# A list scheduler's estimated durations replaced by repeat times, in a kernel of attention, four experts and a gated MLP

## The chip, the cores and the metric

The kernel runs on one core of a Trainium2 chip, in one launch. The metric is the device time of that launch in microseconds, the median of repeated runs. The engines are TensorE (PE; its weight loads are PEld), VectorE (DVE), ScalarE (ACT), GpSimd (POOL) and SyncE (SP), which issues DMAs. Each takes its instructions in program order and waits at semaphores for the others.

## The reference

Three layers follow one another, all in float32. 2 batches of 8 heads, 576 positions, head size 64; then 1152 tokens of 512 numbers.

```python
scores = scale * np.matmul(q, k.transpose(0, 1, 3, 2))
x = (log1p(abs(i - j)) / log1p(max(i, 1)))[..., None]
bias = np.maximum(x @ w1 + b1, 0.0) @ w2          # 32 hidden, one bias per head
attn = softmax(scores + bias); x = attn @ v       # tokens of 8 * 64 numbers
p = domain_probs / (domain_probs.sum(-1, keepdims=True) + 1e-09)
out += p[:, e:e + 1] * (np.maximum(x @ w1[e], 0.0) @ w2[e])   # for 4 experts, 1024 hidden
return ((x @ w_a) * (x @ w_b)) @ w_out            # 1536 hidden, weights in float64
```

## The kernel before

**Operands.** Most matrix products take each float32 operand as a high part and a rest (`hi`, `lo`; `wh`, `wl`; `hh`, `hl`) and add three products of the parts. ScalarE or VectorE makes the high part by a cast, VectorE or GpSimd the rest by a subtraction.

**The bias** (`bias_group`, lines 347 to 409). For each of 36 groups of 16 rows of positions, four operations make the hidden layer `hh` (line 356 on VectorE for three of them, line 358 on ScalarE for one), matmuls make `pb` (line 370), ScalarE or VectorE evacuates one side of it into `bst` (line 388 or 390), GpSimd or ScalarE mirrors the other side (line 395), and SyncE stores the rows in DRAM, `bias_d` (line 405). `bias_tile` (line 448) reads them back as tiles `bt` of 128 rows, two heads at a time. A tile needs all of its eight groups of rows.

**Attention** (`inputs`, `step`, `values`, `group`, lines 429 to 600). Two heads go together. `inputs` loads and splits q and k (lines 438 to 443). A step is a tile of 128 rows: matmuls `ps` (line 490), on VectorE a reduction that adds the bias and finds the row extreme (line 493), on ScalarE the exponential with a sum (line 503), transposes `pt` (line 516), copies into `ptb` (line 234, on ScalarE or VectorE), then for a group of steps the reciprocal sums spread by `rx`, `rp` and `rb` (lines 556 to 570), matmuls `pv` with v (line 581), and the attention's result as `x_hi` and `x_lo` (lines 587 to 590). The first two tiles of batch 0 (256 tokens) come first for all heads: the experts start on them.

**Experts** (`w1_item`, `w2_item`, lines 724 to 753). `up` (line 708) makes the hidden layer of 256 columns, ScalarE applies the relu (line 735), VectorE makes its rest (line 736), `down` (line 719) adds into banks `pz`. Pass 0 has the 256 first tokens, pass 1 all the others, which needs the whole attention. Weights come in 512 KB blocks: load `wst` (line 617), high part and rest (lines 618, 619).

**Gated MLP** (`convert`, `blocks64`, `x2_pair`, `ab_item`, `out_item`, lines 626 to 942). VectorE turns the float64 words into float32 (lines 636 to 657); a scheme with seven products in place of eight makes both up products (`pw`, `pr`, `pq`, line 842), with evacuations into `ct` between them; `out_item` multiplies by `w_out` and adds into `acc` (line 937).

**The order.** Nothing of this is issued as it is written. `op(...)` records an operation with its buffers, a rank (`prio`, lower first) and, for each engine that may do it, an estimated duration in ns. `Plan.run` (line 137) then simulates the engines with these estimates and emits the instructions in the order in which the simulated engines take them; on the chip each engine's queue keeps that order. The rules:

- An engine takes the ready operation of lowest rank, then of greatest age, whose buffers are free. An operation of rank under 0.9 is left to another engine if that one would finish it sooner (line 171).
- On TensorE, expert and MLP matmuls are fill (rank 2). While fill is ready, another matmul is taken only 300 ns after it became ready (MARGIN, line 165).
- A result counts as ready after the duration and a settling time of its engine (SETTLE, line 91).
- A DMA is put at its issue time plus 400 ns, or behind the DMA before it, plus its bytes at 250 per ns, and then 1500 ns more:

```python
dma = max(dma, now + ns + 400) + o.size / self.DMA_RATE
end = dma + self.DMA_LAT - 400
```

The estimates stand in `t_copy` (copies and casts from SBUF), `t_two` (two operands) and `t_psum` (one operand in PSUM), lines 237 to 247, and as numbers in the `op` calls.

Of the kernel before, what the change touches and what calls it, by code (L numbers as in the profile page):

```python
# [226 lines left out]
def tile_kernel(ctx, tc, qd, kd, vd, cst, probs, w1r, w2r, war, wbr, wor, out):  # L227
    nc = tc.nc
# [118 lines left out]
    def bias_group(u, rank):  # L347
# [3 lines left out]
        for g in range(4):  # L351
            G = 4 * u + g
            hh = new("hh")
            hs.append(hh)
            if g < 4 - acts:
                op({"DVE": n / 1.92 + 240}, lambda e, hh=hh, G=G: nc.vector.tensor_scalar(out=hh.t[:, :n], in0=tab[:, :n], scalar1=sc[:, G:G + 1], scalar2=negb, op0=ALU.mult, op1=ALU.max), r=[cs], w=[hh], prio=pri, lock=True)  # L356
            else:
                op({"ACT": n / 1.2 + 390}, lambda e, hh=hh, G=G: nc.scalar.activation(out=hh.t[:, :n], in_=tab[:, :n], func=AF.Relu, scale=sc[:, G:G + 1], bias=cw[:, 1:2]), r=[cs], w=[hh], prio=pri)
        pb = new("tv" if n <= 512 else "s", "pb")
# [11 lines left out]

        op({"PE": n * 1.9 + 350}, mm, r=[*hs, cs], w=[pb], hold=[bst], prio=pri)

# [25 lines left out]
        m = min(before, after - 1)  # L399
        side = op({e: v + 100 for e, v in t_psum(n, ENGINES["side"]).items()}, lambda e: put(e, *ends()[0]), r=[pb, cr], w=[bst], prio=pri)  # L400
        op({e: v for e, v in {"POOL": 2 * m + 150, "ACT": m / 1.2 + 280, "DVE": m / 0.96 + 200}.items() if e in ENGINES["mirror"].split()}, mirror, r=[pb, cr], w=[bst], after=[side], prio=pri)
# [67 lines left out]
    def step(m, b, t, k, q0, Q, K, ptb, sums):  # L469
# [3 lines left out]
        for s in range(2):  # L473
# [32 lines left out]
            if K.room is None:  # L506
                guests.append(o)
            red = op({"DVE": 840}, ttr, r=[ps, bt], hold=[pr, sums])
            if t < 4 or s == 1:
                exps.append(op({"ACT": 970}, ex, after=[red] if t < 4 else [red, half0], w=[sums], hold=[pr]))  # L510
            half0 = red
# [34 lines left out]
    def values(m, b, ts, w, V, ptb, sums):  # L546
# [35 lines left out]

        op({"PE": 10 * w + 350}, pvs, r=[ptb, V, rb], w=[pv], hold=[xf], prio=RANK["pv"])
        c = int(ts[0] > 1)
        o = xcol(b, c) + P * ts[0] - C0 * c
        o = slice(o, o + w)
        op({"DVE": w / 0.96 + 160}, lambda e: nc.vector.tensor_tensor(out=xf.t[:, :w], in0=pv.t[:, :w], in1=rb.t[:, :w], op=ALU.mult), r=[pv, rb], w=[xf], prio=RANK["fin"])
        hi = Buf(t=x_hi)
# [37 lines left out]
    def convert(src, whole):  # L626
# [3 lines left out]
        for h in range(2):  # L630
# [26 lines left out]
            op({"DVE": 690}, lambda e, w0=w0, w1=w1, hl=hl: nc.vector.tensor_tensor(out=hl.t[:, 1], in0=f(w1()), in1=f(w0()), op=ALU.add), r=[st], rw=[hl], prio=RANK["x64"], lock=True)  # L657
            op({"SP": 440}, lambda e, h=h, hl=hl: nc.sync.dma_start(out=wz_d[k, :, :, 512 * h:512 * h + 512].rearrange("a p n -> p a n"), in_=f(hl.t)), r=[hl], w=[done], prio=2, size=524288)
# [36 lines left out]

    EST = {256: 116, 384: 173, 512: 226}
    ups = {}
# [16 lines left out]
    def down(w, z, h, tt, first, final, prio=RANK["fill"], after=()):  # L714
        def mm(e):
            wh, wl = (x.rearrange("p (a b) -> p a b", a=2) for x in w.t)
            for ft in range(2):
                for j, (a, bb) in enumerate(((h.t[0], wh), (h.t[1], wh), (h.t[0], wl))):
                    nc.tensor.matmul(z.t, a[:, ft, tt * P:(tt + 1) * P], bb[:, ft, :], start=(first and ft == 0 and j == 0), stop=(final and ft == 1 and j == 2))  # L719
        op({"PE": 6 * 226}, mm, r=[w, h], w=[z], prio=prio, after=after)  # L720

    WU, ZB = {}, {}

    def w1_item(p, e, c, q):
        t0, nt = CHUNKS[c]
        n = nt * P
        h = new("h1" if p == 0 else "h2", "h")
        if (p, e, q, 0) not in WU:
            WU[p, e, q, 0] = unit(w1r[e, q])
        xs = [X[0, 0]] if p == 0 else list(X.values())[1:]  # L730
        for ft in range(2):
            u, last = up(WU[p, e, q, 0], ft, t0 * P, n, xs, [h])
            for t in range(t0, t0 + nt):
                ups.setdefault(t, []).append(last)
            relu = op({"ACT": n / 1.2 + 170}, lambda en, ft=ft, u=u: nc.scalar.activation(out=h.t[0][:, ft, :n], in_=u.t[:, :n], func=AF.Relu), r=[u], w=[h])  # L735
            op({"DVE": n / 0.96 + 160}, lambda en, ft=ft, u=u: nc.vector.scalar_tensor_tensor(out=h.t[1][:, ft, :n], in0=u.t[:, :n], scalar=0.0, in1=f(h.t[0][:, ft, :n]), op0=ALU.max, op1=ALU.subtract), r=[u], w=[h], after=[relu])  # L736
        return h

    def w2_item(p, e, c, q, h):
# [3 lines left out]
        for tt in range(nt):  # L743
            if q == 0:
                ZB[p, e, c, tt] = new("z", "pz")
            z = ZB[p, e, c, tt]
            down(WU[p, e, q, 1], z, h, tt, q == 0, q == 3)
            t = t0 + tt
            if q == 3:
                if e == 0:  # L750
                    op({"DVE": 745}, lambda en, z=z, t=t: nc.vector.tensor_scalar(out=acc(t), in0=z.t, scalar1=gate[:, t, e:e + 1], scalar2=None, op0=ALU.mult), r=[z, GATE], rw=[ACC[t]])
                else:
                    op({"DVE": 745}, lambda en, z=z, t=t: nc.vector.scalar_tensor_tensor(out=acc(t), in0=z.t, scalar=gate[:, t, e:e + 1], in1=acc(t), op0=ALU.mult, op1=ALU.add), r=[z, GATE], rw=[ACC[t]])

# [63 lines left out]
    def ab_item(q, c):  # L818
# [10 lines left out]
        def prod(j, bank, first, stop, last=(), hold=()):  # L829
            a, x = TERMS[j]  # L830
            got = []
            for m, z in enumerate("ab"):
# [10 lines left out]

                got.append(op({"PE": 6 * (n / 2.4 + 11)}, mm, r=[w, XB[c][x]], w=[bank[m] if type(bank) is tuple else bank], hold=hold, after=last, prio=RANK["fill"]))
            return got
# [58 lines left out]
    def out_item(q, c, h):  # L904
        if (q, "d") not in WU:
            WU[q, "d"] = unit64(UI[q, "d"])
        for tt in range(4 + c):
# [4 lines left out]
            else:  # L912
# [4 lines left out]
                for ft in (1, 0):  # L917
                    for o, w in ((0, 256), (256, 256)) if last and not ft else ((0, 512),):
                        def mm(e, ft=ft, z=z, tt=tt, o=o, w=w):
                            wh, wl = (x.rearrange("p (a b) -> p a b", a=2) for x in WU[q, "d"].t)  # L920
                            for j, (a, bb) in enumerate(((h.t[0], wh), (h.t[1], wh), (h.t[0], wl))):
                                nc.tensor.matmul(z.t[:, o:o + w], a[:, ft, tt * P:(tt + 1) * P], bb[:, ft, o:o + w], start=(ft == 1 and j == 0), stop=(ft == 0 and j == 2), skip_group_check=last)  # L922
                        got.append(op({"PE": 3 * (w / 2.4 + 13)}, mm, r=[WU[q, "d"]], w=[z], hold=[h], prio=RANK["fill"], after=[*parts[q, c, ft], *got[-1:]]))
                if last:
                    for i, g in enumerate(got[1:]):
                        cols = slice(256 * i, 256 * i + 256)
                        x = op({"DVE": 430}, lambda e, z=z, t=t, cols=cols: nc.vector.tensor_tensor(out=acc(t)[:, cols], in0=z.t[:, cols], in1=acc(t)[:, cols], op=ALU.add), after=[g, *ACC[t].writers], hold=[z, ACC[t]], prio=RANK["evac2"])

# [5 lines left out]
            if q == 0:  # L934
                op({"ACT": 600}, lambda e, z=z, t=t: nc.scalar.copy(acc(t), z.t), r=[z], rw=[ACC[t]], prio=RANK["evac2"])
            else:
                op({"DVE": 745}, lambda e, z=z, t=t: nc.vector.tensor_tensor(out=acc(t), in0=z.t, in1=acc(t), op=ALU.add), r=[z], rw=[ACC[t]], prio=RANK["evac2"])
            if q == NQ - 1:
# [178 lines left out]
```

## Time and profile before

| | before |
|---|---|
| median of 3 runs | 833.38 us (832.92 to 834.51) |
| span of the profiled execution | 829.8 us |
| instructions | 12737 |
| TensorE busy | 802.7 us (97%), 4859 matmuls |
| VectorE busy | 627.3 us (76%) |
| ScalarE busy | 352.5 us (42%) |
| GpSimd busy | 43.5 us (5%) |
| moved by DMA | 128.13 MB |

The span goes from the first to the last instruction of one profiled execution; the time of a run is 3.6 us longer in the median. The ends of matmuls are modelled and overlap: a busy TensorE need not be at its pace. Durations of VectorE and ScalarE overlap at their ends as well, so that the time from start to start (the repeat time) is shorter than the duration of one. The stages in order of time are: bias and attention alone (to about 92 us), attention with pass 0 of the experts beside it (to 294), pass 1 (to 574), and the gated MLP.

### The profile page before, as it was taken

How to read it: one execution, taken by the hardware profiler on the slowest of the kernel's cores; microseconds unless marked ns; L12 is line 12 of the kernel's file. 1: busy time of each engine (PE TensorE's matmuls, PEld its weight loads, DVE VectorE, ACT ScalarE, POOL GpSimd, SP SyncE). 2: the span in 40 equal slices, each digit the busy share in tenths (PEclk: the TensorE clock that was granted, in tenths of full speed). 3: DMA queues.
4: the chain of work that ended last, by engine and by line, in shares of the span. 5: the costliest groups of instructions: out<-in, count | busy, mean ns of one | idle time of the engine just before them, and what ended most of it. 6: DMA issues, size and time to landing. Idle time of an engine off the chain costs nothing.

```text
span 829.8 us, 12737 instructions
## 1 busy us (share of the span) xinstructions
PE 802.7 (97%) x4859; PEld 668.8 (81%) x4859; DVE 627.3 (76%) x1232; ACT 352.5 (42%) x696; POOL 43.5 (5%) x62
## 2 busy tenths in 40 slices
PE   7778999999999999999999999999999999999997
PEld 2446776898897788889888988888888999899996
DVE  7998999788888768787888787875556665747545
ACT  6677877477676611132122212213345432323211
POOL 1002100000110000000000000000010001100000
PEclk9999999999999999999999999999999999999999
DMA  6989877575656444556465555640302221211103
GB/s 225 311 286 355 280 242 249 195 238 189 222 176 213 131 164 120 185 176 206 115 199 194 164 141 169 224 126 2 101 1 87 67 66 37 77 31 47 51 2 114
DMA packets 48589, 128.13 MB, mean 154 GB/s; under 512 B 5136, under 2 KB 9488, under 8 KB 48528
## 3 DMA queue, kind: packets, MB, share of 16 engines
q1 hardware_dynamic: 48384, 127.18, 47.5%
q8 instruction: 38, 0.62, 0.3%
q14 instruction: 23, 0.19, 0.1%
q10 hardware_dynamic: 144, 0.13, 0.0%
HBM read 101.46 MB, written 25.84 MB: 153 GB/s over the span
## 4 chain that ended last, share of the span: by engine, by line
PE 90%; DVE 5%; DMA 3%; ACT 1%; issue 1%; DVEq 0%
PE pz L719 32%; PE up L708 24%; PE pw L842 9%; PE ps L490 5%; PE pv L581 4%; PE pr L842 4%; PE pt L516 4%; PE pq L842 2%; PE pb L370 2%; DMA k<-in_kd 1%; DVE hh L356 1%; PE pz L922 1%; DMA bt<-bias_d 1%; ACT pr L503 1%; DMA bias_d<-bst 1%
## 5 line engine op out<-in xcount | busy, mean ns | idle before, releaser
L719 PE MATMUL pz<-wh,hh 128*128 128x512 f32 x386 | 154.0, 399 | 0.0
L719 PE MATMUL pz<-wl,hh 128*128 128x512 f32 x386 | 152.3, 395 | 0.0
L719 PE MATMUL pz<-wh,hl 128*128 128x512 f32 x386 | 151.6, 393 | 0.0
L708 PE MATMUL up<-x_hi,wh 128*128 128x256 f32 (+2 forms) x384 | 133.1, 347 | 0.4 <-DVE hl L736 0.4
L708 PE MATMUL up<-x_hi,wl 128*128 128x256 f32 (+2 forms) x384 | 129.8, 338 | 0.0
L708 PE MATMUL up<-x_lo,wh 128*128 128x256 f32 (+2 forms) x384 | 129.7, 338 | 0.0
L735 ACT ACTIVATE hh<-up 128x256 fp32r<-128x256 f32 (+2 forms) x96 | 47.1, 491 | 141.7 <-PE up L708 141.2
L234 ACT CAST wh<-wst 128x1024 fp32r<-128x1024 f32 (+1 forms) x66 | 66.4, 1007 | 91.0 <-PE pz L719 71.4
L719 PEld LDWEIGHTS pz<-wl,hh 128*128 128x128 f32 x386 | 72.5, 188 | 17.2
L619 DVE TENSOR_TENSOR wl<-wst,wh 128x1024 fp32r<-128x1024 f32 x64 | 78.0, 1222 | 9.9 <-ACT wh L234 9.6
L719 PEld LDWEIGHTS pz<-wh,hh 128*128 128x128 f32 x386 | 72.6, 188 | 15.0 <-issue 0.7
L719 PEld LDWEIGHTS pz<-wh,hl 128*128 128x128 f32 x386 | 72.6, 188 | 14.7
L708 PEld LDWEIGHTS up<-x_hi,wh 128*128 128x128 f32 x384 | 72.4, 188 | 9.5 <-issue 1.6
L708 PEld LDWEIGHTS up<-x_lo,wh 128*128 128x128 f32 x384 | 72.4, 189 | 6.5
L708 PEld LDWEIGHTS up<-x_hi,wl 128*128 128x128 f32 x384 | 72.3, 188 | 5.9
L736 DVE SCALAR_TENSOR_TENSOR hl<-up,hh 128x256 fp32r<-128x256 f32 (+2 forms) x96 | 53.0, 554 | 29.3 <-ACT hh L735 28.8
L234 ACT COPY ct<-pw 128x512 f32<-128x512 f32 (+3 forms) x48 | 27.8, 579 | 108.0 <-PE pw L842 100.6
L493 DVE CUSTOM_DVE_ANT_0 pr<-ps,bt 128x576 f32<-128x576 f32 (+1 forms) x80 | 59.7, 754 | 10.9 <-PE ps L490 8.4
L503 ACT ACTIVATE pr<-pr,sums 128x576 f32<-128x576 f32 x72 | 55.9, 776 | 12.5 <-DVE sums L493 11.7
L370 PE MATMUL pb<-hh,cs 128*32 128x288 f32 (+17 forms) x352 | 46.6, 497 | 6.6 <-DVE hh L356 5.1
L356 DVE TENSOR_SCALAR hh<-cs,negb 128x576 f32<-128x576 f32 (+17 forms) x108 | 49.1, 504 | 0.2
L516 PE MATMUL pt<-ident,pr 128*128 128x128 f32 x288 | 43.6, 280 | 2.6 <-ACT pr L503 2.4
(161 smaller groups left out, 1415.6 us busy)
## 6 DMA issues: line engine op xcount, KB each, us to landing
wst<-in_w1r SPq DMA_DIRECT2D x32, 512.0 KB, 4.1
wst<-in_w2r SPq DMA_DIRECT2D x32, 512.0 KB, 4.3
bt<-bias_d SPq DMA_DIRECT2D x24, 576.0 KB, 5.7
bias_d<-bst SPq DMA_DIRECT2D x36, 295.5 KB, 4.7
k<-in_kd SPq DMA_DIRECT2D x16, 576.0 KB, 4.9
v<-in_vd SPq DMA_DIRECT2D x20, 320.0 KB, 4.9
s<-in_war SPq DMA_DIRECT2D x12, 512.0 KB, 5.1
wz_d<-hl SPq DMA_DIRECT2D x24, 256.0 KB, 2.5
```

What stands on the lines that cost most here:

```text
L234: (nc.scalar.copy if e == "ACT" else engine[e].tensor_copy)(out, in_)
L356: op({"DVE": n / 1.92 + 240}, lambda e, hh=hh, G=G: nc.vector.tensor_scalar(out=hh.t[:, :n], in0=tab[:, :n], scalar1=sc[:, G:G + 1], scala ...
L370: nc.tensor.matmul(t[32 * g:32 * g + 32, o + lo:o + hi], w2s, hs[g].t[:, lo:hi], start=True, stop=True)
L493: nc.vector.tensor_tensor_reduce(out=pr.t[r0:r1, c].rearrange("p (a b) -> p a b", a=2), in0=ps.t[r0:r1, :, :HS], in1=bt.t[r0:r1, c].rearra ...
L503: nc.scalar.activation(out=pr.t[:, c], in_=pr.t[:, c], func=AF.Exp, scale=-1.0, bias=sums.t[:, neg:neg + 1], accum_out=sums.t[:, col:col + 1])
L516: nc.tensor.transpose(pt.t[:, kt * P:kt * P + P], pr.t[:, s, k0:k0 + P], ident)
L619: op(t_two(1024, ENGINES["wlo"]), lambda e: engine[e].tensor_tensor(out=w.t[1], in0=wst.t, in1=f(w.t[0]), op=ALU.subtract), r=[wst], rw=[w ...
L708: nc.tensor.matmul(u.t[:, :n], a[:, d, ft * P:(ft + 1) * P], x[:, d, lo:lo + n], start=(d == 0 and j == 0), stop=(d == 3 and j == 2))
L719: nc.tensor.matmul(z.t, a[:, ft, tt * P:(tt + 1) * P], bb[:, ft, :], start=(first and ft == 0 and j == 0), stop=(final and ft == 1 and j = ...
L735: relu = op({"ACT": n / 1.2 + 170}, lambda en, ft=ft, u=u: nc.scalar.activation(out=h.t[0][:, ft, :n], in_=u.t[:, :n], func=AF.Relu), r=[u ...
L736: op({"DVE": n / 0.96 + 160}, lambda en, ft=ft, u=u: nc.vector.scalar_tensor_tensor(out=h.t[1][:, ft, :n], in0=u.t[:, :n], scalar=0.0, in1 ...
L842: nc.tensor.matmul(o_, s[:, k], d[:, k], start=(first and k == 0 and i == 0), stop=(k == 1 and i == 2), skip_group_check=True)
```

## The change

Every estimate that the diff touches becomes smaller, but for those of the expert and MLP matmuls, which grow by 1 to 3%, and three settling times, which grow by 20 to 40 ns. DMA estimates, ranks, buffers, engine lists and the arithmetic stay. The first two parts of the diff:

```diff
-    SETTLE = {"PE": 190, "ACT": 110, "DVE": 110, "POOL": 120}
+    SETTLE = {"PE": 210, "ACT": 150, "DVE": 140, "POOL": 120}
...
     def t_copy(n, engs="ACT DVE"):
-        est = {"ACT": n / 1.2 + 170, "DVE": n / 1.92 + 170, "POOL": n + 100}
+        est = {"ACT": n / 1.2 + 95, "DVE": n / 1.92 + 68, "POOL": n + 100}
...
     def t_two(n, engs="POOL DVE"):
-        est = {"POOL": 2.17 * n + 170, "DVE": n / 0.96 + 160}
+        est = {"POOL": 2.17 * n + 140, "DVE": n / 0.96 + 68}
...
     def t_psum(n, engs="ACT DVE"):
-        est = {"ACT": n / 1.2 + 170, "DVE": n / 0.96 + 160}
+        est = {"ACT": n / 1.2 + 55, "DVE": n / 0.96 + 68}
```

The rest are numbers in `op` calls (ns; n and w are columns):

| line | operation | before | after |
|---|---|---|---|
| 356 | bias `hh` on VectorE | n / 1.92 + 240 | n / 1.92 + 190 |
| 358 | bias `hh` on ScalarE | n / 1.2 + 390 | n / 1.2 + 285 |
| 372 | bias matmuls `pb` | 1.9 n + 350 | 1.67 n + 250 |
| 400 | bias evacuation, added to `t_psum` | 100 | 95 |
| 508 | score reduction | 840 | 690 |
| 510 | exponential | 970 | 770 |
| 583 | `pv` matmuls | 10 w + 350 | 8.35 w + 170 |
| 587 | `xf` | w / 0.96 + 160 | w / 0.96 + 68 |
| 647, 648, 651 | float64 conversion | 840, 1110, 1110 | 790, 1060, 1060 |
| 653, 657 | float64 conversion, sums | 690 | 605 |
| 696 | `up` matmul of 256, 384, 512 columns | 116, 173, 226 | 119, 174, 231 |
| 720 | `down`, six matmuls | 6 x 226 | 6 x 231 |
| 735 | relu | n / 1.2 + 170 | n / 1.2 + 68 |
| 736 | rest of the hidden layer | n / 0.96 + 160 | n / 0.96 + 68 |
| 751, 753 | expert's sum | 745 | 663 |
| 844, 923 | MLP matmuls, added to each | 11, 13 | 14, 14 |
| 927, 935, 937 | MLP's sum | 430, 600, 745 | 335, 482, 600 |

Unchanged are, among others, `ps` (560 ns), the transposes (440), SyncE's issue (440), the mirrors, the 400 ns of the last tile's `rb`, and every number of DMAs.

## Rows read from the trace of the kernel before

**Rows 1.** The page: busy us (share of the span) and instructions of each engine.

```profile
PE 802.7 (97%) x4859; PEld 668.8 (81%) x4859; DVE 627.3 (76%) x1232; ACT 352.5 (42%) x696; POOL 43.5 (5%) x62
```

**Rows 2.** Busy time by stretch: us, PE, PEld, DVE, ACT, POOL, PEclk, DMA share, GB/s.

```profile
0.00:92.00 92.00, 74.03 (x594) 43.32 (x595) 83.38 (x217) 66.89 (x137) 10.73 (x25) 0.98 0.87 300
92.00:294.00 202.00, 200.08 (x1457) 161.99 (x1456) 170.41 (x347) 138.38 (x294) 13.44 (x16) 1.00 0.64 206
294.00:600.00 306.00, 306.00 (x1420) 259.87 (x1421) 237.98 (x413) 72.74 (x115) 4.99 (x3) 1.00 0.49 153
600.00:830.00 230.00, 222.61 (x1393) 203.59 (x1391) 135.51 (x256) 74.54 (x152) 14.36 (x19) 1.00 0.16 52
```

**Rows 3.** The chain of waits from 290 to 330 us: start us, us, what.

```profile
293.91 8.52 PE up L708 x48
302.43 5.60 PE pz L719 x24
```

**Rows 4.** The chain of waits from 52 to 92 us.

```profile
54.32 4.44 DMA bias_d<-bst
...
58.77 6.75 DMA bt<-bias_d
...
91.49 0.59 PE up L708 x5
```

**Rows 5.** TensorE's waits over the whole span: us in total, times, longest us.

```profile
PE pb L370 <- DVE hh L356: 5.1, 7, 1.8
...
PE ps L490 <- DVE sums L493: 4.1, 2, 2.6
...
PE pw L842 <- DVE x_lo L812: 1.0, 1, 1.0
PE pw L842 <- DVE ct L867: 1.0, 6, 0.2
```

**Rows 6.** VectorE from 4 to 8 us in order of time, then its group by shape.

```profile
4.20 3.00 DVE L356 TENSOR_SCALAR hh<-cs,negb 128x576 f32<-128x576 f32 x6
...
L356 DVE TENSOR_SCALAR hh<-cs,negb 128x576 f32<-128x576 f32 x6 | 3.1, 580 | 0.0
```

**Rows 7.** The chain of waits from 0 to 140 us: ScalarE's exponentials.

```profile
34.21 1.63 ACT pr L503 x4
```

**Rows 8.** VectorE's groups of instructions from 0 to 92 us: busy us, mean ns, idle before.

```profile
L356 DVE TENSOR_SCALAR hh<-cs,negb 128x416 f32<-128x416 f32 (+17 forms) x78 | 34.0, 491 | 0.1
L493 DVE CUSTOM_DVE_ANT_0 pr<-ps,bt 128x576 f32<-128x576 f32 x22 | 16.0, 753 | 2.2 <-DMA bt<-bias_d 1.6 <-PE ps L490 0.5
L234 DVE COPY ptb<-pt 128x512 f32<-128x512 f32 (+1 forms) x14 | 7.1, 510 | 0.1
```

**Rows 9.** ScalarE's groups of instructions from 0 to 92 us.

```profile
L358 ACT ACTIVATE hh<-cs 128x416 f32<-128x416 f32 (+17 forms) x26 | 18.6, 729 | 1.9 <-DVE cs L323 1.9
L388 ACT ACTIVATE bst<-pb,corr 128x384 f32<-128x384 f32 (+25 forms) x34 | 17.7, 560 | 10.3 <-PE pb L370 4.4 <-PE ps L490 2.6 <-issue 1.6
L503 ACT ACTIVATE pr<-pr,sums 128x576 f32<-128x576 f32 x21 | 16.2, 773 | 4.1 <-DVE sums L493 3.9
L234 ACT COPY ptb<-pt 128x512 f32<-128x512 f32 (+1 forms) x16 | 7.6, 498 | 1.8 <-PE pt L516 1.7
```

**Rows 10.** Busy time by stretch of 2 us, columns as in rows 2.

```profile
64.00:66.00 2.00, 0.00 (x0) 0.00 (x0) 0.44 (x2) 2.00 (x5) 0.40 (x1) 1.00 1.05 407
66.00:68.00 2.00, 1.52 (x7) 1.52 (x8) 1.97 (x6) 2.00 (x4) 0.42 (x1) 0.72 1.05 402
68.00:70.00 2.00, 2.00 (x12) 1.98 (x11) 1.97 (x4) 1.05 (x4) 1.96 (x1) 0.50 1.02 393
```

**Rows 11.** The page's DMA issues: KB each, us to landing.

```profile
bt<-bias_d SPq DMA_DIRECT2D x24, 576.0 KB, 5.7
bias_d<-bst SPq DMA_DIRECT2D x36, 295.5 KB, 4.7
```

**Rows 12.** Waits of all engines from 0 to 80 us.

```profile
DVE pr L493 <- DMA bt<-bias_d: 1.6, 1, 1.6
```

More of the change, by code (lines that the diff above doesn't have):

```diff
@@ L399, in bias_group @@
         m = min(before, after - 1)
-        side = op({e: v + 100 for e, v in t_psum(n, ENGINES["side"]).items()}, lambda e: put(e, *ends()[0]), r=[pb, cr], w=[bst], prio=pri)
+        side = op({e: v + 95 for e, v in t_psum(n, ENGINES["side"]).items()}, lambda e: put(e, *ends()[0]), r=[pb, cr], w=[bst], prio=pri)
         op({e: v for e, v in {"POOL": 2 * m + 150, "ACT": m / 1.2 + 280, "DVE": m / 0.96 + 200}.items() if e in ENGINES["mirror"].split()}, mirror, r=[pb, cr], w=[bst], after=[side], prio=pri)
@@ L507, in step @@
                 guests.append(o)
-            red = op({"DVE": 840}, ttr, r=[ps, bt], hold=[pr, sums])
+            red = op({"DVE": 690}, ttr, r=[ps, bt], hold=[pr, sums])
             if t < 4 or s == 1:
-                exps.append(op({"ACT": 970}, ex, after=[red] if t < 4 else [red, half0], w=[sums], hold=[pr]))
+                exps.append(op({"ACT": 770}, ex, after=[red] if t < 4 else [red, half0], w=[sums], hold=[pr]))
             half0 = red
@@ L586, in values @@
         o = slice(o, o + w)
-        op({"DVE": w / 0.96 + 160}, lambda e: nc.vector.tensor_tensor(out=xf.t[:, :w], in0=pv.t[:, :w], in1=rb.t[:, :w], op=ALU.mult), r=[pv, rb], w=[xf], prio=RANK["fin"])
+        op({"DVE": w / 0.96 + 68}, lambda e: nc.vector.tensor_tensor(out=xf.t[:, :w], in0=pv.t[:, :w], in1=rb.t[:, :w], op=ALU.mult), r=[pv, rb], w=[xf], prio=RANK["fin"])
         hi = Buf(t=x_hi)
@@ L656, in convert @@
             op(t_two(512, ENGINES["s64"]), lambda e, w1=w1, hl=hl: engine[e].tensor_tensor(out=f(w1()), in0=f(w1()), in1=f(hl.t[:, 0]), op=ALU.subtract), r=[hl], rw=[st], prio=RANK["x64"], lock=True)
-            op({"DVE": 690}, lambda e, w0=w0, w1=w1, hl=hl: nc.vector.tensor_tensor(out=hl.t[:, 1], in0=f(w1()), in1=f(w0()), op=ALU.add), r=[st], rw=[hl], prio=RANK["x64"], lock=True)
+            op({"DVE": 605}, lambda e, w0=w0, w1=w1, hl=hl: nc.vector.tensor_tensor(out=hl.t[:, 1], in0=f(w1()), in1=f(w0()), op=ALU.add), r=[st], rw=[hl], prio=RANK["x64"], lock=True)
             op({"SP": 440}, lambda e, h=h, hl=hl: nc.sync.dma_start(out=wz_d[k, :, :, 512 * h:512 * h + 512].rearrange("a p n -> p a n"), in_=f(hl.t)), r=[hl], w=[done], prio=2, size=524288)
@@ L694, in acc @@
         return acc_t[t]
-    EST = {256: 116, 384: 173, 512: 226}
+    EST = {256: 119, 384: 174, 512: 231}
     ups = {}
@@ L842, in mm @@
                             nc.tensor.matmul(o_, s[:, k], d[:, k], start=(first and k == 0 and i == 0), stop=(k == 1 and i == 2), skip_group_check=True)
-                got.append(op({"PE": 6 * (n / 2.4 + 11)}, mm, r=[w, XB[c][x]], w=[bank[m] if type(bank) is tuple else bank], hold=hold, after=last, prio=RANK["fill"]))
+                got.append(op({"PE": 6 * (n / 2.4 + 14)}, mm, r=[w, XB[c][x]], w=[bank[m] if type(bank) is tuple else bank], hold=hold, after=last, prio=RANK["fill"]))
             return got
@@ L926, in out_item @@
                         cols = slice(256 * i, 256 * i + 256)
-                        x = op({"DVE": 430}, lambda e, z=z, t=t, cols=cols: nc.vector.tensor_tensor(out=acc(t)[:, cols], in0=z.t[:, cols], in1=acc(t)[:, cols], op=ALU.add), after=[g, *ACC[t].writers], hold=[z, ACC[t]], prio=RANK["evac2"])
+                        x = op({"DVE": 335}, lambda e, z=z, t=t, cols=cols: nc.vector.tensor_tensor(out=acc(t)[:, cols], in0=z.t[:, cols], in1=acc(t)[:, cols], op=ALU.add), after=[g, *ACC[t].writers], hold=[z, ACC[t]], prio=RANK["evac2"])
                         def put(e, t=t, cols=cols, i=i):
@@ L934, in out_item @@
             if q == 0:
-                op({"ACT": 600}, lambda e, z=z, t=t: nc.scalar.copy(acc(t), z.t), r=[z], rw=[ACC[t]], prio=RANK["evac2"])
+                op({"ACT": 482}, lambda e, z=z, t=t: nc.scalar.copy(acc(t), z.t), r=[z], rw=[ACC[t]], prio=RANK["evac2"])
             else:
-                op({"DVE": 745}, lambda e, z=z, t=t: nc.vector.tensor_tensor(out=acc(t), in0=z.t, in1=acc(t), op=ALU.add), r=[z], rw=[ACC[t]], prio=RANK["evac2"])
+                op({"DVE": 600}, lambda e, z=z, t=t: nc.vector.tensor_tensor(out=acc(t), in0=z.t, in1=acc(t), op=ALU.add), r=[z], rw=[ACC[t]], prio=RANK["evac2"])
             if q == NQ - 1:
```

28 lines of the change are left out of this document (14 added, 14 removed).

## The prediction

> **What bounds the kernel now.** I read the page's busy times first [rows 1]. TensorE is busy for 97% of the span and VectorE for 76%, so the kernel looks bound by matmuls. The share is an average over stages, so the next view is busy time by stretch [rows 2]. Four stages stand out. From 0 to 92 us TensorE is busy for 74.0 of 92 us, VectorE for 83.4 and ScalarE for 66.9. From 92 to 294 us TensorE is idle for 202 - 200.1 = 1.9 us. From 294 to 600 us it is idle for nothing. From 600 us to the end it is idle for 7.4 us, part of which is the last store. The chain of waits shows what full means [rows 3]: the piece that starts at 293.91 lasts 8.52 us and the next starts at 302.43, which is the sum. Forty-eight matmuls of mixed widths follow one another with no gap, and no order of the same matmuls makes that stretch shorter.
>
> So the schedule can gain or lose in two places: the first 92 us, where there is no expert matmul yet to put into a gap, and, by small amounts, the ends of the other stages. In the first stage VectorE is the fullest engine (83.4 of 92, 91%) while ScalarE has 25 us to spare. The chain there holds one long wait [rows 4]: a bias row block is stored to DRAM for 4.44 us and read back as a bias tile for 6.75 us, 11.2 us in a row, in which TensorE runs dry. TensorE's own waits say the same [rows 5]: 5.1 us for VectorE's `hh` and 4.1 us for `sums` in the early part, and after 600 us waits of 1.0 and 1.0 us as the largest two.
>
> **The change part by part.** No arithmetic changes and no buffer. Each operation gets another estimated duration, and the planner emits another order for all five queues, with another choice of engine where it has one. The matmuls, DMAs and bytes are the same in number, so the edits cost nothing by themselves; everything comes from the order.
>
> *Whether the new figures are right.* Six `hh` operations of 576 elements take 3.00 us in one run on VectorE, one of which lasts 580 ns [rows 6]. The first five starts are thus (3.00 - 0.58) / 5 = 0.484 us apart. The old estimate is 576 / 1.92 + 240 = 540 ns, the new one 490 ns. On ScalarE two exponentials with their two accumulator reads take 1.63 us [rows 7], 0.815 us each with the tail of the last one, against 970 before and 770 now. The new numbers are the pace that the chip keeps. The page "VectorE: DVE Perf Modes" of the Trainium skill, section "The DRAIN you can't avoid", says that the next operation does not start until the pipe of the one before is empty; by it the pace would be the full 580 ns and the new figure 90 ns short. The row's 484 ns speaks against that, and the row decides here.
>
> *How wrong the old plan was in the first stage.* VectorE ran 78 `hh`, 22 score reductions and 14 probability copies there [rows 8]. The diff takes 50, 150 and some 92 ns from them: 3.9 + 3.3 + 1.3 = 8.5 us, and about 5 us more over the other 80 or so (of 217 [rows 2]) at some 60 ns each, so some 13.4 us of 83.4, or 16%. ScalarE ran 26 `hh`, 34 `bst`, 21 exponentials and 16 copies [rows 9], from which the diff takes 105, up to 120, 200 and 115 ns: 2.7 + 4.1 + 4.2 + 1.8 = 12.8 us of 66.9, or 19%. The old plan made both engines too slow, ScalarE rather more. Operations of low rank take the engine that would finish first, so the plan has been sending VectorE some work that ScalarE had time for.
>
> *Term 1, VectorE relieved in the first stage.* The 14 copies cost 7.1 us [rows 8]. For 512 elements ScalarE's estimated lead over VectorE grows from 96 to 119 ns, and its estimated backlog shrinks by 19%. The bounds are 0 (nothing moves, or narrow copies move back as reciprocal spreads do, whose lead on VectorE grows) and 7.1 us (all move). I take a third, 2.4 us, since both backlogs shrink and the lead alone tips only close cases. VectorE is 91% full and on the chain's DMA trip through `hh`, so I count what it sheds in full: **-2.4 us**.
>
> *Term 2, the clock.* TensorE does nothing from 64 to 66 us; the granted clock then stands at 0.72 and 0.50 of 2.4 GHz in the next two stretches of 2 us, so at 1.2 GHz for part of them [rows 10]. That loses 2 x 0.28 + 2 x 0.50 = 1.6 us. If the store goes out earlier or the hole holds other matmuls, this goes; if it only moves, it stays. Bounds 0 and 1.6; I take half: **-0.8 us**.
>
> *Term 3, 92 to 294 us.* The attention steps lie between expert matmuls there. Idle time is 1.9 us [rows 2]; a tighter plan frees `pr`, `ptb` and the banks earlier, but leaves less slack for each hand-over. The planner still holds an attention matmul back for 300 ns after it is ready if there is a fill (MARGIN), which is more than the 50 to 200 ns that each estimate loses. Bounds -1.9 and +1.9; I take **-0.9 us**, since the matmuls of this stage have fill beside them.
>
> *Term 4, 294 us to the end.* Up to 600 us there is nothing to gain and VectorE has slack (238 of 306 us busy [rows 2]): **0**. After that the products wait a little for ScalarE's and VectorE's evacuations; the two largest waits are 2.0 us together [rows 5]. The settling time of these engines goes up by 40 and 30 ns as the duration goes down by 115 and 92, so the hand-over is expected some 60 to 75 ns sooner. Bounds -2.0 and +2.0; I take 0, the middle, since the products have a fixed order.
>
> The weight splits, the bias load and the queue of SyncE are moved with the rest. Their cost is in the bounds: SyncE issues in plan order, and what stands behind an issue that waits for a buffer waits too. GpSimd gets a little less, since VectorE's estimate falls more (92 ns) than its own (30 ns); it is busy for 5% [rows 1] and that weighs nothing.
>
> **The sum.** -2.4 - 0.8 - 0.9 + 0 = -4.1 us. The profiled execution's span is 829.8 us and would be 825.7. The median of the runs is 833.4, 3.6 us above the span, which I add again: 829.3 us. A measurement of this kernel can tell 0.2%, 1.7 us, from no change.
>
> **The rivals.**
>
> *A: nothing measurable.* The first stage is set by VectorE's total work and by the two DMA trips, the rest by matmuls. If no copy changes its engine, terms 1 and 2 are zero and the time is 833.4 - 0.9 = 832.5. For it: 306 us without any gap [rows 3], and DMA estimates that the change does not touch. Against it: the first 92 us have a lot of air, and another order will hardly give the same sum. Chance 0.13.
>
> *B: slower, late DMAs unmasked.* The planner's formula gives a bias store of 0.30 MB 0.44 + 0.40 + 1.21 + 1.50 = 3.55 us and a bias load of 0.59 MB 4.70 us, 8.25 together. The chain took 11.2 us [rows 4], and the median landings are 4.7 and 5.7 us [rows 11]. The plan is 2.9 us early at this trip. So far compute estimates 16 to 19% too long covered 11.2 x 0.16 = 1.8 us of that; with true compute times the cover is gone, and the in-order queues meet the data late. Today VectorE waits 1.6 us for that tile at the head of its queue [rows 12]; all that stands behind, the next reductions and `hh`, waits too, and TensorE for them. The price is 2.9 us at this trip and another 1.6 us of clock after a longer hole: +4.5, so 837.9 us. It decides if VectorE's wait for `bt` grows beyond the 2.4 us that term 1 gives. Against it: a wait there can be filled with `hh` of the later bias groups, which need no DMA. Chance 0.30.
>
> *C: the pipe empties between VectorE operations.* Then the new figures would be too short by about 90 ns on each. Over the 217 instructions of the first stage [rows 2] the plan would miss 19.5 us of VectorE's work; if a fifth of them stand where TensorE waits, that is 3.9 us: 837.3 us. This is the drain rule of the same page of the Trainium skill; the 0.484 us pace [rows 6] speaks against it. Chance 0.02.
>
> *D: the change does not do what it says.* Where a new figure is no repeat time after all (an operation that waits on its neighbour more often than the row shows), the plan is early there. That would cost what B costs in another place, at most the 1.9 us of idle time in the second stage once more and the 2.0 us of the last: 837.3 us. Chance 0.03.
>
> **How the numbers follow.** My forecast has 0.52. Faster by over 0.2% is 0.52; A gives 0.13 for no change; B, C and D together 0.35 for slower. The forecast's own range goes from all bounds at their best, 7.1 + 1.6 + 1.9 = 10.6 us less, 822.8, to 831.7, where it becomes no change. The whole range reaches up through B with the doubled idle times of the later stages (837.9 + 1.9 + 2.0 = 841.8), of which I leave out the last tenths: 822.5 to 841.5.
>
> **What would show it.** Right: fewer `ptb` copies on VectorE before 92 us, the first expert matmul some 2 to 4 us earlier than at 91.5 [rows 4], the clock at full where it was 0.50, and 294 to 600 us as gapless as before. Wrong: a longer wait of VectorE for `bt`, a second hole of TensorE in the first stage, or idle time of TensorE before `pw` in the last stage well above now. If the time moves by more than 10 us either way, the order has found or lost something that I have not seen here.

## The result, and the profile after

The kernel after takes 842.62 us (841.1 to 843.46, 4 runs) beside 833.15 us (832.34 to 834.51, 4 runs) of the kernel before: ratio 1.0108, 95% interval 1.0093 to 1.0123. It is slower by 9.5 us; the forecast was 4.1 us faster, and the time lies above the range. The span of the profiled execution is 839.3 us.

The page's busy times, as [rows 1]:

```profile
PE 804.7 (96%) x4859; PEld 670.7 (80%) x4859; DVE 627.3 (75%) x1229; ACT 349.5 (42%) x703; POOL 44.3 (5%) x58
```

Work has not grown: the same matmuls, and nearly the same sums for VectorE and ScalarE. So the 9.5 us are waiting time or clock. Busy time by stretch, as [rows 2] (us; PE, PEld, DVE, ACT, POOL; PEclk, DMA share, GB/s):

```profile
0.00:92.00 92.00, 68.56 (x536) 39.90 (x540) 79.20 (x202) 60.31 (x125) 6.38 (x18) 0.94 0.82 273
92.00:294.00 202.00, 196.73 (x1452) 158.95 (x1445) 170.76 (x346) 136.42 (x303) 9.00 (x16) 1.00 0.65 210
294.00:600.00 306.00, 306.00 (x1440) 259.53 (x1439) 237.44 (x415) 74.59 (x119) 15.06 (x9) 1.00 0.49 153
600.00:840.00 240.00, 233.41 (x1439) 212.32 (x1438) 139.90 (x267) 78.23 (x159) 13.82 (x15) 1.00 0.17 57
```

In the first 92 us all three engines do less than before: TensorE 5.5 us, VectorE 4.2, ScalarE 6.6. From 294 to 600 us TensorE is as full as it was. The chain of waits gives the marks that answer to [rows 3, 4]:

```profile
67.37 5.21 DMA bt<-bias_d
...
100.90 0.91 PE up L708 x6
...
305.06 8.33 PE up L708 x48
313.38 5.60 PE pz L719 x24
```

The same marks, taken from the trace's order of time, are the measure for every run below: the issue of the 16th bias store (the last that the second tile of attention needs; pass 0 waits for the first two tiles), the first expert matmul (the first fill), the first matmul of pass 1, the first MLP product `pw` and the last matmul.

| us | 16th store | first fill | pass 1 | first `pw` | last matmul |
|---|---|---|---|---|---|
| before | 54.3 | 91.3 | 293.8 | 604.4 | 825.7 |
| after | 60.2 | 100.8 | 304.9 | 615.1 | 835.2 |

The loss is 9.5 us up to the first fill and 1.6 us from there to pass 1; then 0.4 and 1.2 us come back. Of the first part, 5.9 us are there when the 16th store goes out. VectorE makes three of the four `hh` for it; its busy time from 24 us to that store, first of before, then of after (columns as above):

```profile
24.00:54.30 30.30, 24.60 (x210) 14.99 (x208) 29.42 (x80) 22.53 (x51) 1.17 (x3) 1.00 0.90 323
```

```profile
24.00:60.20 36.20, 27.43 (x212) 16.58 (x210) 31.09 (x84) 24.05 (x53) 1.77 (x4) 0.93 0.81 290
```

Before, VectorE is idle for 30.30 - 29.42 = 0.9 us; after, for 36.20 - 31.09 = 5.1 us, and it does 1.7 us more work ahead of the store: 4.2 + 1.7 = 5.9. VectorE in order of time shows such idle time (start us, us, what, idle before and releaser). Before:

```profile
38.56 0.74 DVE L234 CAST x_hi<-k 128x1152 fp32r<-128x1152 f32 x1
...
39.53 0.76 DVE L493 CUSTOM_DVE_ANT_0 pr<-ps,bt 128x576 f32<-128x576 f32 x1
...
41.01 1.36 DVE L443 TENSOR_TENSOR x_hi<-k,x_hi 64x1152 fp32r<-64x1152 f32 x1
```

After:

```profile
31.16 2.46 DVE L356 TENSOR_SCALAR hh<-cs,negb 128x400 f32<-128x400 f32 x6
33.53 0.75 DVE L234 CAST x_hi<-k 128x1152 fp32r<-128x1152 f32 x1
34.31 1.35 DVE L443 TENSOR_TENSOR x_hi<-k,x_hi 64x1152 fp32r<-64x1152 f32 x1
35.70 1.23 DVE L356 TENSOR_SCALAR hh<-cs,negb 128x368 f32<-128x368 f32 x3
...
39.31 0.17 DVE L556 TENSOR_SCALAR sums<-sums 128x2 f32<-128x2 f32 x1 [1.02 <-ACT pr L503]
...
40.69 0.29 DVE L234 COPY ptb<-pt 128x128 f32<-128x128 f32 x1 [0.76 <-PE pt L533]
41.65 0.76 DVE L493 CUSTOM_DVE_ANT_0 pr<-ps,bt 128x576 f32<-128x576 f32 x1 [0.67 <-PE ps L490]
```

Before, a split of k stands among the first attention steps and fills VectorE while the others answer. After, that split is done ahead of them, and VectorE waits for ScalarE and TensorE at the head of its queue, 2.5 us here, with `hh` queued behind.

Not all of the 5.9 us comes through the store's own `hh` (those of 336 columns) on VectorE. Before, then after:

```profile
47.92 0.81 DVE L356 TENSOR_SCALAR hh<-cs,negb 128x336 f32<-128x336 f32 x2
...
52.17 0.77 PE L370 MATMUL pb<-hh,cs 128*32 128x336 f32 x8
```

```profile
51.96 1.18 DVE L356 TENSOR_SCALAR hh<-cs,negb 128x336 f32<-128x336 f32 x3
...
58.43 0.77 PE L370 MATMUL pb<-hh,cs 128*32 128x336 f32 x8
```

These `hh` end at 48.7 and 53.1 us, 4.4 us later, but their `pb` start 6.3 us later: on TensorE they stand behind transposes that wait for ScalarE's exponentials.

Nor is the store the last word. After, it lands 2.3 us after its issue, at 62.5 us, where the one before took 4.4 us [rows 4]. The load of the second tile, which needs it, still goes out only at 67.37, because SyncE issues in the planned order and a load of weights and a store of a later bias group stand ahead of it:

```profile
bias_d<-bst SPq DMA_DIRECT2D x1, 295.5 KB, 2.3
```

```profile
65.88 0.33 SPq L617 DMA_DIRECT2D wst<-in_w1r  x1
66.26 1.00 SPq L405 DMA_DIRECT2D bias_d<-bst  x1
67.37 1.55 SPq L458 DMA_DIRECT2D bt<-bias_d  x3
```

Before, the store landed at 54.32 + 4.44 = 58.76 and the load went out at 58.77 [rows 4]. So the 9.5 us up to the first fill are 5.9 at the store's issue and 4.9 on SyncE's queue, less 2.2 and 1.5 for the faster store and load, and 2.4 behind the load's landing.

The waits up to 102 us (us, times, longest), first TensorE, then VectorE, then ScalarE, answer to [rows 5, 12]:

```profile
PE pb L370 <- DVE hh L356: 7.8, 8, 2.4
PE pt L516 <- ACT pr L503: 6.6, 2, 4.0
PE ps L490 <- DVE sums L493: 3.5, 1, 3.5
```

```profile
DVE pr L493 <- DMA bt<-bias_d: 2.4, 1, 2.4
DVE sums L556 <- ACT pr L503: 2.0, 4, 1.0
```

```profile
ACT bst L388 <- PE pb L370: 8.8, 7, 3.3
ACT bst L388 <- DMA bias_d<-bst: 8.1, 5, 2.7
```

The clock falls three times where it fell once [rows 10]. Busy time by 10 us around the first fall, and by 2 us in the other two, columns as above:

```profile
20.00:30.00 10.00, 6.82 (x27) 1.63 (x28) 9.39 (x18) 5.03 (x10) 1.76 (x4) 0.83 0.65 193
...
38.00:40.00 2.00, 1.30 (x7) 1.09 (x8) 0.85 (x5) 1.86 (x5) 0.00 (x0) 0.79 1.06 409
40.00:42.00 2.00, 2.00 (x11) 2.00 (x10) 0.64 (x2) 0.59 (x1) 0.00 (x0) 0.50 1.03 414
42.00:44.00 2.00, 2.00 (x25) 1.51 (x23) 1.70 (x8) 1.21 (x4) 0.00 (x0) 0.85 1.02 416
...
72.00:74.00 2.00, 0.46 (x2) 0.46 (x3) 1.28 (x3) 1.83 (x3) 0.00 (x0) 0.83 0.93 256
74.00:76.00 2.00, 2.00 (x10) 1.98 (x10) 1.97 (x7) 1.21 (x5) 0.00 (x0) 0.50 0.96 354
```

### The profile page after: what moved, and what is told of

Same layout as the page of the kernel before. It is cut to its first block, busy times and chain, and to the rows that moved or that the text cites. A ratio compares the mean times of both kernels' runs of the same rounds, so it can differ in the third digit from the quotient of the medians.

```text
span 839.3 us, 12747 instructions
## 1 busy us (share of the span) xinstructions
PE 804.7 (96%) x4859; PEld 670.7 (80%) x4859; DVE 627.3 (75%) x1229; ACT 349.5 (42%) x703; POOL 44.3 (5%) x58
## 4 chain that ended last, share of the span: by engine, by line
PE 84%; DVE 9%; DMA 3%; ACT 3%; issue 1%; SPq 0%; DVEq 0%
PE pz L719 31%; PE up L708 23%; PE pw L842 9%; PE pv L581 4%; PE ps L490 4%; PE pr L842 4%; PE pt L516 3%; PE pq L842 2%; DVE hh L356 2%; PE pb L370 2%; DMA k<-in_kd 1%; DVE pr L493 1%; DVE k L443 1%; ACT pr L503 1%; PE pz L922 1%
## 5 line engine op out<-in xcount | busy, mean ns | idle before, releaser
L234 ACT CAST wh<-wst 128x1024 fp32r<-128x1024 f32 (+1 forms) x62 | 62.3, 1006 | 84.3 <-PE pz L719 71.8
```

Of the source, the lines that this page charges most:

```text
L234: (nc.scalar.copy if e == "ACT" else engine[e].tensor_copy)(out, in_)
```

## The experiments

Each ratio below is against runs of the kernel before on the same chip.

### Which figures matter: the late ones, the early ones, one group alone

First the kernel before with only the new figures of the float64 conversions, experts and MLP (lines 647 to 937), and the kernel after with those put back:

```diff
-    EST = {256: 116, 384: 173, 512: 226}
+    EST = {256: 119, 384: 174, 512: 231}
...
-        op({"PE": 6 * 226}, mm, r=[w, h], w=[z], prio=prio, after=after)
+        op({"PE": 6 * 231}, mm, r=[w, h], w=[z], prio=prio, after=after)
```

> The kernel before with only the new figures of the float64 conversion, the experts and the MLP. Order theory (the loss is in the order of the first 300 us, which the front figures set): the first expert matmul stays at 91.3 us within 0.5, time 833 to 836 us. Late-figures theory (the expert and MLP figures cost the time): 840 us or more, with the first 92 us as before.

> The changed kernel with the figures of the float64 conversion, the experts and the MLP put back. Order theory: the first expert matmul near 100.8 us as in the changed kernel, time 840 to 848 us. Late-figures theory: 833 to 835 us.

Late figures alone: 837.97 us, ratio 1.0057 (1.0042 to 1.0073). Early ones alone: 849.34 us, 1.0198 (1.0179 to 1.0217). The first stage follows the early figures: first fill at 91.5 and 102.5 us. The rest isn't additive: the first kernel loses 4.4 us between first fill and pass 1 (206.9 us against 202.5) though its first stage is the old one, and the second loses 7.5 us there (210.0). So the two groups together (842.62) are better than the early one alone. The order theory had the first fills right, but both times came out above its ranges of 833 to 836 and 840 to 848 us.

Attention's four figures alone (lines 508, 510, 583, 587) on the kernel before:

```diff
-            red = op({"DVE": 840}, ttr, r=[ps, bt], hold=[pr, sums])
+            red = op({"DVE": 690}, ttr, r=[ps, bt], hold=[pr, sums])
...
-                exps.append(op({"ACT": 970}, ex, after=[red] if t < 4 else [red, half0], w=[sums], hold=[pr]))
+                exps.append(op({"ACT": 770}, ex, after=[red] if t < 4 else [red, half0], w=[sums], hold=[pr]))
```

> The kernel before with the new figures of the attention alone (score reduction, exponential, pv, xf: four lines). Hole theory: with these alone the plan of VectorE and ScalarE in the first stage is 3.3 + 4.2 us looser, so a good part of the delay is there: first expert matmul 95 to 101 us, 836 to 845 us. If the bias and copy figures are what matters: 91 to 93 us.

839.49 us, 1.0078 (1.0064 to 1.0093): first fill at 103.9 us, later than with all figures new, and then the shortest middle stretch of all, 198.6 us. Four numbers are enough to upset the first stage.

### Is it the truth of the figures, or any other order?

Every estimate times a random factor of its own between 0.98 and 1.02, three draws on the kernel before and three on the kernel after:

```diff
+        rnd = random.Random(SEED * 100003 + len(self.ops))
+        eng = {k: v * (1 + 0.02 * (2 * rnd.random() - 1)) for k, v in eng.items()}
```

> The kernel before with every estimate multiplied by its own random number from 0.98 to 1.02 (seed 0). No figure is truer or less true than before. Luck theory (the old figures gave one of the best orders near them, and any redraw loses some of it): 836 to 844 us, clearly slower than before. Figures theory (what counts is that the old figures were too long and the new ones are not): within 2 us of before, 831 to 836 us, first expert matmul within 1.5 us of 91.3.

> The same with seed 1. Luck theory: 836 to 844 us. Figures theory: 831 to 836 us.

> Kernel before, every estimate times an own random factor from 0.98 to 1.02, a third draw. If the kernel before is a lucky draw of its neighbourhood: 836 to 847 us, first expert matmul to pass 1 about 210 us as in the two draws before it (210.7, 210.0) and not 202.5. If its place is no luck: 831 to 835 us.

> The changed kernel with every estimate multiplied by its own random number from 0.98 to 1.02 (seed 0). Luck theory: the changed kernel is an ordinary draw, so noise moves it little and to either side, 838 to 847 us, first expert matmul from 96 to 104 us. If noise as such harms (a plan with true figures is better than one with false ones): above 845 us, as it did to the kernel before (846.95 and 838.83).

> The same with seed 1: 838 to 847 us by the luck theory; above 845 us if noise as such harms.

> Kernel after, every estimate times an own random factor from 0.98 to 1.02, a third draw, to set three draws around the new figures (two so far: 842.5 and 839.7 us) beside three around the old ones (847.0, 838.8, 844.6 us). If the new figures are no worse than the old ones and only the kernel before was a lucky order: 837 to 847 us. If true figures are the worse ones as such: 845 us or more.

| us (ratio) | time | first fill | to pass 1 |
|---|---|---|---|
| old figures, draw 0 | 846.95 (1.0177, 1.015 to 1.0204) | 97.4 | 210.7 |
| old, draw 1 | 838.83 (1.0073, 1.0058 to 1.0088) | 92.1 | 210.0 |
| old, draw 2 | 844.63 (1.0142, 1.011 to 1.0174) | 93.9 | 209.8 |
| new figures, draw 0 | 842.5 (1.0118, 1.0097 to 1.0139) | 103.2 | 203.0 |
| new, draw 1 | 839.74 (1.0091, 1.006 to 1.0121) | 98.7 | 202.4 |
| new, draw 2 | 844.86 (1.0143, 1.0124 to 1.0162) | 101.8 | 205.2 |

This is the main reading of the study. Factors of 2% that mean nothing cost the old figures 6 to 14 us, and move the new ones by no more than 2.9 us either way. The means are 843.5 us for the old figures and 842.4 for the new; the three draws of each set are spread over 8.1 and 5.1 us, so a difference of a few us between the sets is neither shown nor ruled out. The kernel after lies in the middle of the six; the kernel before lies 6.1 us below the best of them on the same chip. Old draw 0 lost more than the luck theory's 844 us allowed; the other five lie in its ranges. The old figures have the earlier first fill, the new ones the shorter stretch behind it; of these eight kernels only the one before has both, 91.3 and 202.5. In the three new draws SyncE holds the load of the second tile for less than 0.1 us after its store has landed, and the first fill is late all the same: that hold belongs to the one order of the kernel after.

### Late DMAs, buffers, the choice of engine

Three edits of the kernel after: the planner's DMA latency raised, a fourth `bst` buffer, and the casts of weights, k and the bias side kept off VectorE:

```diff
-    DMA_LAT = 1900
+    DMA_LAT = 2700
```

> The changed kernel in which the planner's DMA latency is 2700 ns in place of 1900, so that a bias store and load come out at about the 11.2 us that the chain showed less than 1.4. Late-DMA theory (rival B of the prediction: true compute figures unmask DMAs that the plan expects too early): the first expert matmul returns to 91 to 95 us and the time to 833 to 837 us. Hole theory: no better, first expert matmul 97 to 104 us, 839 to 847 us.

```diff
-    place(R["bst"], hp, "bst", 3, [P, S + 16])
+    place(R["bst"], hp, "bst", 4, [P, S + 16])
```

> The changed kernel with four buffers of bias rows in place of three. ScalarE waits for a bias store to land 8.1 us in total before 102 us in the changed kernel and 1.2 in the kernel before. Late-DMA theory: with another buffer that wait goes, and the first expert matmul comes 4 us or more earlier than 100.8. Hole theory: the wait moves to the next hand-over, first expert matmul within 3 us of 100.8, 839 to 846 us.

```diff
-ENGINES = {"kcast": "ACT DVE", "ksub": "POOL DVE", "qcast": "DVE", "qsub": "POOL DVE", "pt": "ACT DVE", "tail": "ACT DVE", "side": "ACT DVE", "mirror": "POOL ACT",
-           "whi": "ACT DVE", "wlo": "DVE", "xhi": "DVE", "xlo": "POOL DVE", "rb": "ACT DVE", "rx": "ACT DVE", "s64": "POOL DVE",
+ENGINES = {"kcast": "ACT", "ksub": "POOL DVE", "qcast": "DVE", "qsub": "POOL DVE", "pt": "ACT DVE", "tail": "ACT DVE", "side": "ACT", "mirror": "POOL ACT",
+           "whi": "ACT", "wlo": "DVE", "xhi": "DVE", "xlo": "POOL DVE", "rb": "ACT DVE", "rx": "ACT DVE", "s64": "POOL DVE",
```

> The changed kernel in which the casts of weights and of k and the bias evacuation are left to ScalarE alone, so that VectorE does none of them. Engine theory (VectorE got casts in the first 100 us that ScalarE did before, 3 weight casts for 1): the first expert matmul comes 2 us or more earlier than 100.8, time 838 to 840 us. Hole theory (VectorE waits at the head of its queue for hand-overs that the plan puts just in time): within 1 us of 100.8, time 841 to 845 us.

None helps: 843.37 us (1.0123, 1.0108 to 1.0139), 842.09 (1.0107, 1.0093 to 1.012) and 844.93 (1.0142, 1.0118 to 1.0166), with first fills at 102.7, 105.4 and 104.3 us. The last two come later than either theory allowed. With the longer latency VectorE waits more for `bt`, not less:

```profile
DVE pr L493 <- DMA bt<-bias_d: 4.0, 1, 4.0
```

With four buffers ScalarE's wait for a store's landing is gone (8.1 us after) and its wait for `pb` takes its place (8.8 us after):

```profile
ACT bst L388 <- PE pb L370: 14.7, 13, 3.1
...
ACT bst L388 <- DMA bias_d<-bst: 0.7, 1, 0.7
```

The 16th store then goes out at 49.7 us, the earliest of all, with only six score reductions ahead of it, where the kernel before and the one after have all eight of the first tile. Yet the first fill comes latest of these three: the load of the second tile stands on SyncE behind a later store, which goes out at 60.84 us:

```profile
61.25 1.61 SPq L458 DMA_DIRECT2D bt<-bias_d  x1
```

With the casts away from VectorE, its busy time up to 92 us falls to 72.36 us, and its idle time up to the store rises:

```profile
24.00:62.40 38.40, 28.48 (x215) 19.01 (x212) 30.26 (x80) 24.00 (x51) 2.80 (x5) 0.87 0.79 270
```

That is 8.1 us idle. VectorE's amount of work alone isn't what sets the first stage.

### What keeps VectorE from running dry?

A theory of holes: with estimates that are too long VectorE and ScalarE never run dry in the plan, and so not on the chip; with true ones the plan hands over just in time. The kernel after with the front (bias and attention) estimates of both engines multiplied by 1.3, and with that only for the first 16 bias groups and 10 attention groups:

```diff
+        if self.front:
+            eng = {k: v * 1.3 if k in ('ACT', 'DVE') else v for k, v in eng.items()}
```

```diff
+        plan.front = u < 16
...
+        plan.front = n < 10
```

> The changed kernel with the estimates of VectorE and ScalarE for the bias and attention multiplied by 1.3, the rest as changed: far too long, more than in the kernel before. Hole theory: in the plan these engines never run dry, so it packs other ready work between a step and its successor, and the first expert matmul comes near 91 us again (88 to 94); what the total does is open, 836 to 848 us, since the stretch from there to pass 1 is drawn anew. Theory that true figures are better where they are used: later than 100.8 us and above 845 us.

> The changed kernel with VectorE's and ScalarE's estimates multiplied by 1.3 for the first 16 bias groups and the first 10 attention groups alone, new figures everywhere else. Hole theory together with the sums so far (first expert matmul at 89.9 with all front figures x 1.3; 202 to 204 us from there to pass 1 in every kernel with all new figures; 310.2 and 220.1 us after that): last matmul near 90 + 203 + 310 + 220 = 823 us, time 829 to 835 us, equal to or a little faster than before. If long figures at the start only shift the loss: above 838 us.

840.76 us (1.0097, 1.0077 to 1.0118) and 834.72 us (1.0014, 1.0002 to 1.0025), with first fills at 89.9 and 92.4 us. VectorE's stretch from 24 us to the 16th store, in each:

```profile
24.00:51.20 27.20, 24.77 (x191) 14.64 (x192) 26.23 (x71) 19.56 (x44) 4.51 (x8) 0.94 0.92 329
```

```profile
24.00:50.90 26.90, 24.17 (x186) 14.25 (x186) 26.43 (x70) 19.37 (x42) 5.92 (x8) 0.94 0.94 325
```

Idle for 1.0 and 0.5 us, and the first fill is back near 91.3 us. With false figures to the end of attention the middle takes 214.3 us, 10.2 more than after; with false ones at the start only, 205.5. The second kernel is 1.2 us slower than the kernel before on the same chip: nearly all of the 9.5 us come back, and nothing more.

If the length did it, half the lengthening should do half, and shortening should harm:

> Kernel after with the estimates of ScalarE and VectorE in bias and attention multiplied by 1.15 (half the way to the run with 1.3; later figures true). First expert matmul so far: 98.7 to 105.4 us in the kernels with true front figures, 89.9 to 97.4 in those with too long ones. Hole theory (the length matters, by degrees): first expert matmul between, 93 to 98 us; the stretch from there to pass 1 204 to 212 us; the kernel 836 to 841 us. Luck-of-the-draw theory (any change of figures redraws the order, the length itself counts for nothing): the first expert matmul is as likely at 99 to 105 us as below.

> Kernel after with the same estimates multiplied by 0.85, too short. Hole theory: the plan has more holes than with true figures, first expert matmul at 103 us or later, the kernel at 843 us or above. Luck-of-the-draw theory: first expert matmul anywhere from 90 to 105 us.

848.03 us (1.0171, 1.0152 to 1.0189) and 852.79 us (1.0229, 1.0206 to 1.0252): first fill at 100.8 and 100.9 us. There is no half step; with 0.85 the stretch to pass 1 takes 213.0 us, and the kernel is worse in all. With 1.15 the stretch to the store again has 4.0 us idle:

```profile
24.00:59.60 35.60, 26.62 (x221) 17.83 (x220) 31.55 (x87) 22.48 (x45) 3.75 (x5) 0.90 0.84 293
```

So the length of the estimates by itself does not decide. Last, the hand-over alone: true durations, and 200 or 400 ns more of settling time for bias and attention results.

```diff
-                        end = now + ns + self.SETTLE[e]
+                        end = now + ns + self.SETTLE[e] + (200 if o.front else 0)
```

> Kernel after, durations untouched; only the settling time of bias and attention results (what the plan allows for a hand-over between engines) is 200 ns longer. Hand-over theory (the plan with true durations hands results over just in time, the in-order queues on the chip wait, and VectorE stands idle with other work queued behind): the 16th bias store goes out some 2 to 5 us earlier than at 60.2 us, VectorE's idle time from 24 us to that store falls from 5.1 to 2 to 4 us, first expert matmul 96 to 100 us, the kernel 836 to 842 us. Draw theory (any other order will do as well or as badly): the store anywhere from 50 to 63 us, no tie to the idle time.

> The same with 400 ns. Hand-over theory: VectorE's idle time from 24 us to the 16th bias store under 2 us, the store at 50 to 56 us, first expert matmul at 90 to 97 us, the kernel 832 to 840 us (the middle stretch may give 200 to 212 us). Draw theory: no further step in the same direction than with 200 ns.

845.8 us (1.0147, 1.0132 to 1.0162) and 866.68 us (1.0388, 1.037 to 1.0407). The stretch to the store, with 200 and with 400 ns:

```profile
24.00:57.30 33.30, 26.50 (x195) 16.21 (x195) 31.13 (x82) 21.91 (x48) 4.83 (x7) 0.93 0.89 316
```

```profile
24.00:59.50 35.50, 26.35 (x200) 15.68 (x195) 31.39 (x85) 21.02 (x42) 4.17 (x8) 0.95 0.83 280
```

With 200 ns the idle time falls to 2.2 us and the store comes 2.9 us earlier, as that theory expected; but the first fill gains only 0.8 us and the stretch behind it loses 4.7. With 400 ns the idle time is back at 4.1 us, the first fill comes at 107.7 us and the middle takes 222.9. The theory fails as a rule: neither setting makes the order good.

**What is settled and what is open.** Settled: the loss arises before pass 1. In all twenty kernels the stretch from pass 1 to the first `pw` takes 310 to 314 us and the one behind it 219 to 224; the times differ by what lies ahead. In the kernel after, the 16th store is late by its own `hh` and by the wait of its `pb` on TensorE, and the load behind it by the order of SyncE's queue. The old figures' order was a favourable draw: each of three redraws loses 6 us or more, and none of the nineteen other kernels is faster. Open: which decision of the planner begins the bad start. The moved split of k above is one candidate, the place of the load in SyncE's queue another; neither was tried alone.

## Why the prediction was wrong, point by point

**The pace.** This step held for `hh`. The run of six `hh` from 31.16 us takes 2.46 us after; by shape they are (busy us, mean ns, idle before)

```profile
L356 DVE TENSOR_SCALAR hh<-cs,negb 128x400 f32<-128x400 f32 x3 | 1.3, 476 | 0.0
L356 DVE TENSOR_SCALAR hh<-cs,negb 128x384 f32<-128x384 f32 x3 | 1.3, 472 | 0.0
```

The starts are (2.46 - 0.47) / 5 = 0.398 us apart; the new figure for these widths is 400 / 1.92 + 190 = 398 ns and 390 ns. Rival C, the pipe that empties between operations, is out for `hh` in a row: the starts are closer than the 472 to 476 ns of one. The prediction gave only half of the passage that it cites. The Trainium skill, "VectorE: DVE Perf Modes", section "The DRAIN you can't avoid", says that the next operation does not start until the pipe is empty, and in the same paragraph that a next operation which is not held back starts earlier. The rows of `hh`, 0.398 us from start to start, agree with the second sentence. Rival D is out by the same rows for `hh`, VectorE's most frequent operation there.

Behind the subtraction of k it is otherwise. The one at 34.31 us above lasts 1.35 us and the next `hh` start at 35.70, 1.39 us after its start; the old figure was 1152 / 0.96 + 160 = 1360 ns, the new one is 1268. There C and D are right, by 0.12 us on each of six such subtractions up to the first fill, 0.7 us in all.

**Term 1, the step that failed.** I said that VectorE sheds copies worth 2.4 us, "so I count what it sheds in full". Up to the first fill, first before (14 copies of 7.1 us), then after with its copies and its casts of weights:

```profile
0.00:91.30 91.30, 73.33 (x588) 42.62 (x589) 82.68 (x216) 66.19 (x136) 10.62 (x24) 0.98 0.87 299
```

```profile
0.00:100.80 100.80, 74.93 (x592) 43.80 (x592) 86.86 (x222) 66.58 (x139) 7.45 (x20) 0.95 0.83 278
```

```profile
L234 DVE COPY ptb<-pt 128x512 f32<-128x512 f32 (+1 forms) x10 | 5.2, 525 | 1.0 <-PE pt L533 0.8
...
L234 DVE CAST wh<-wst 128x1024 fp32r<-128x1024 f32 x3 | 2.1, 685 | 0.0
```

It did shed copies, 1.9 us of them. But other work came in their place, three casts of weights for one among it, so that VectorE is busy for 4.2 us more, and it is idle for 13.9 us instead of 8.6, 5.3 more. The stage became 4.2 + 5.3 = 9.5 us longer. Work shed from a nearly full engine counts only if nothing takes its place and its queue stays fed. Taking more work off it (the casts) made the idle time worse. The order of SyncE's queue, which holds the load for 4.9 us, was in the prediction too ("what stands behind an issue that waits for a buffer waits too"), but as part of the bounds, with no number.

**Behind that stands an assumption that no term carried:** that an order planned with truer times is better than the one at hand, and that the order at hand is a typical one. I priced the change as the old order with small parts moved. The six draws show no gain in the mean from truer figures, and the order at hand was no typical one: each of its three redraws is slower by 6 us or more.

**Term 2, the clock,** had the wrong sign. The clock falls three times instead of once; up to 92 us it is 0.94 against 0.98, that is some 0.06 x 92 = 5.5 us of lost clock against 0.02 x 92 = 1.8, not all of it on the path.

**Term 3** (-0.9) became +1.6 us, inside its bounds of 1.9. But its bounds were taken from idle time before; in the other kernels this stretch moved by -3.9 to +20.4 us, the widest spread of any stretch. **Term 4** (0) held: -0.4 and -1.2 us.

**Rival B** had the sign, and its price of 4.5 us was half the loss; its mechanism was not it. VectorE's wait for `bt` is 2.4 us, up by 0.8, at the point from which B was to decide and not beyond it; transfers land about as before (median 4.9 us for a store and 5.5 for a load, against 4.7 and 5.7 [rows 11]); and telling the planner of slower DMAs mended nothing. The load that sets the stage is late by its place in SyncE's queue and by the late issue of its store, which lands sooner than before. **Rival A** fell to the measured interval.

## What to carry to other kernels

The order that this greedy list scheduler made was a draw: where it stands among its neighbours is found by redrawing it with a per cent or two of noise, before any change of its figures is priced. Here truer figures moved the mean of three draws by 1.1 us, less than the draws differ among themselves, and lost the good draw at hand. And relief of a full engine is worth something only where its in-order queue stays fed; look at its idle time up to the hand-over that sets the stage, and at what stands ahead of that hand-over in the other queues, not at its share of busy time.

## What was not expected of the hardware

In the first stage after the change TensorE's granted clock fell three times, each time about the end of a hole in TensorE's work: of 2.4 us (up to 21.4), 4.0 us (up to 38.7) and 3.5 us (up to 73.5), the longest waits in the rows above. Another hole, of 2.5 us up to 57.0, was followed by no fall. In the windows of 2 us the second and third fall take the same course: 0.79 or 0.83, then 0.50 (1.2 GHz), and 0.85 after the second. That is 2 x (0.21 + 0.50 + 0.15) = 1.7 us of clock, as are the 10 x 0.17 us of the first, much like the 1.6 us of the one before [rows 10]: where TensorE is on the path, this comes on top of the hole.
